# G from split operands in row tiles beside the first MLP, hi and lo of w4 in one matmul, and w4's pages in order of use

## The chip, the cores and the metric

The kernel runs on one core of one Trainium2 chip. The time is the device time of one execution in microseconds; for the kernel before it is the median of three runs. The engines of the core are named as in the profile: PE (TensorE, with its weight loads as PEld), DVE (VectorE), ACT (ScalarE), POOL (GpSimd) and SP (the queue that issues the DMAs).

## The reference

Attention reads between tokens and a small state, both ways, and then two MLPs over all 4352 tokens (8 batches of 512 tokens and 32 state rows, 512 wide).

```python
scores = scale * np.matmul(x, state.transpose(0, 1, 3, 2))      # B=8, H=8, S=512, Ns=32, D=64
a = softmax(scores)
xread = np.matmul(a, state)
a2 = softmax(scale * np.matmul(state, x.transpose(0, 1, 3, 2)))
sread = np.matmul(a2, x)
x = concat([xread, sread], axis=2)            # to 4352 x 512
h = np.maximum(x @ moe_w_in, 0.0)             # 512 -> 2048
x = h * h @ moe_w_out                         # 2048 -> 512
h = x @ moe2_w_in                             # 512 -> 2048
return (h * (1.0 / (1.0 + np.exp(-h)))) @ moe2_w_out
```

The four weight matrices arrive as 64-bit floats and are converted on the chip from their words.

## The kernel before, in words

**Accuracy.** A product of two float32 matrices is built from operands split into a hi part (rounded to the matmul type fp32r) and a lo part (the rest): hi x hi, hi x lo and lo x hi, three matmuls. `split_into` makes the parts, the hi cast on ACT and the subtraction on DVE or POOL. A few small products are done as plain F32 matmuls instead, which take longer per column.

**Order.** The kernel is written as a list of operations in class `Plan`: each call on an engine is recorded with its operands, the dependences are derived, and a greedy list scheduler orders each engine's instructions by urgency with costs from `cost` and by the slot in which the operation was recorded. Every recorded call is made in one helper, so all instructions have the line L185 in the profile; tiles tell them apart. The tiles live in 50 pages of 128x1024 floats, 10 quads of 128x512 floats, and eight banks of the accumulator memory, two each of psA, psB, psC and psD (`BA` to `BD` in the code).

**Stages.** (1) The words of a weight pair (`c_load`, `c_abs`, `c_bits`) become a float32 page by `c_sum`, or hi and lo by `c_split`. (2) The attention read xread is folded into the first MLP: `g_unit` computes G = state x w_in for a quarter q of the 2048 columns and a pair of heads, in 16 units (two for each of the eight pairs of w1); it writes G of the first two batches straight into their pages `Glo`, the rest to memory, from where `G_load` brings it back. (3) `scores` makes the attention scores; for the first three batches (b < NB = 3) as F32 matmuls against `sblkf`, a block diagonal copy of the state that `s_put` fills; for later ones from split parts. Softmax and transposes run on DVE and ACT and give AT, split into AThi and ATlo. (4) The first MLP runs in slots, one slot for a batch j and a chunk c of 128 of the 2048 columns: `gemm1` (six matmuls of 512 columns into psC, from G and AT), relu and square in `chain_a` (tile gact), and two slots later `gemm2` (twelve matmuls into psA and psB). The first three batches run their chunks 0 to 7 first and then 8 to 15, so that the conversion of the weights can keep up. The last slots serve the state rows, for which `w1_load` brings w1 back from memory and splits it. (5) The second MLP uses the seven products of Strassen and Winograd: `gemm3` in five units of tokens with four steps pp each, through silu to the tensors t in memory, and `gemm4` for pairs q of token blocks (q = 0 to 7, and a half pair 8).

**gemm4 before.** The operand tiles `g..hi`, `g..lo` (loaded and split by `g_op`, for pair q, product i and half h) are the stationary side, the pages w4 (hi and lo next to each other, 256 columns each) stream. For each of the products 1, 6, 2, 7, 5, 4, 3, each token block b of the pair and each of eight chunks k, three matmuls of 256 columns are issued, g hi with w hi, g hi with w lo and g lo with w hi, all into one half of a bank. The banks alternate with q. Products 1 and 2 share bank psA: the sum of product 1 is copied to the tile u (ACT) before product 2 adds to the same bank; DVE adds the rest into u and into the output tiles z0 and z1, which SP stores.

**Pages of w4.** `w4_load(pp)` loads all seven product pages of row block jj = pp ahead of step pp of the last gemm3 unit; they are split inside gemm4's first pair.

Of the kernel before, what the change touches and what calls it, by code (L numbers as in the profile page):

```python
# [27 lines left out]
class Plan:  # L28
# [78 lines left out]
    def cost(self, eng, method, writes, reads, args):  # L107
# [12 lines left out]
        if eng == "pe":  # L120
            n = 1
            for d in writes[0].shape[1:]:
                n *= d
            if method == "transpose":
                return 109
            share = 4 if args.get("tile_position") else 1
            return max(n / 2.4 + 13, 109) * (4 if args["rhs"].dtype == F32 else 1) / share
# [249 lines left out]
def attn_moe_moe_kernel(  # L377
# [46 lines left out]
    w1_d = [dram_tile([P, 1024], f"w1d{i}") for i in range(NC // 2)]  # L424
# [3 lines left out]
    g_d = [[dram_tile([4, P] + k + [512], f"g{i}{q}") for i, k in enumerate(([], [2]))] for q in range(4)]  # L428
# [129 lines left out]
    st = plan.tile(pages, [P, 4, 4, 2, NS], F32, "page", "st")  # L558
    sblk = [page(f"sblk{i}") for i in range(2)]
    sblkf = [quad(f"sblkf{b}") for b in range(NB)]  # L560
# [3 lines left out]
    def st_of(b, r):  # L564
        return st[r * 64:(r + 1) * 64, b // 2, :, b % 2].rearrange("p (g l) n -> p g l n", l=2)
# [10 lines left out]
    def s_put(b, dst, a):  # L576

        v = dst.rearrange("p (g a c) -> p g a c", g=2, a=4)
        for r in range(2):
            ps = slice(r * 64, (r + 1) * 64)  # L580
            copy(v[ps, :, a, r * NS:(r + 1) * NS], st_of(b, r))

# [3 lines left out]
    def g_unit(i):  # L586
        q, p = divmod(i, 4)
        g, l = divmod(p, 2)
        pg = w1p[("w1", i // 2)][:, i % 2 * 512:(i % 2 + 1) * 512]
        for bp in range(0, 4, 2):  # L590
            ts = [acc_tile(bp), acc_tile(bp + 1)]
            for k in range(2):
                for r in range(2):
                    ps, co = slice(r * 64, (r + 1) * 64), 64 * (r ^ k)
                    T.matmul(out=ts[k][co:co + 64], lhsT=st[ps, bp + k, p].rearrange("p e n -> p (e n)"),
                             rhs=pg[ps], start=True, stop=True, tile_position=(r * 64, co))
            o2 = page(f"go{i}{bp}", F32).rearrange("p (k f) -> p k f", k=2)
            for k in range(2):
                copy(o2[:, k], ts[k])
            if bp == 0:  # L600
                for b in range(2):
                    if (b, q) not in gp:
                        gp[(b, q)] = [None, page(f"Glo{b}{q}")]
                    for r in range(2):
                        D.dma_start(f32(gp[(b, q)][1])[l * 64 + r * NS:l * 64 + (r + 1) * NS, g * 512:(g + 1) * 512],
                                    o2[r * 64 + b * NS:r * 64 + (b + 1) * NS, 0])
                D.dma_start(g_d[q][0][p], o2[:, 1])
            else:
                D.dma_start(g_d[q][1][p], o2)

    def w1_store(i):
        D.dma_start(w1_d[i], w1p.pop(("w1", i)))

    def w1_load(i):
        w1p[("s", i)] = split_page(f"w1s{i}", 1024, lambda lo: D.dma_start(lo, w1_d[i]))

    def G_load(b, q):
        lo = page(f"Glo{b}{q}")
        bp, e = divmod(b, 2)
        src = g_d[q][1][:, :, bp % 2] if bp > 1 else g_d[q][0]  # L620
        for l in range(2):
            for r in range(2):
                ro = (r ^ bp % 2) * 64 + e * NS
                po = l * 64 + r * NS
                D.dma_start(f32(lo)[po:po + NS].rearrange("p (g f) -> p g f", g=2),
                            src.rearrange("(g l) x f -> l x g f", l=2)[l, ro:ro + NS])
# [21 lines left out]
    def scores(b, g):  # L648
# [280 lines left out]
    def w4_load(jj):  # L929

        w4p[jj] = {}
        for i in SEQ4:
            w4p[jj][i] = page(f"w4{jj}_{i}")
            lo = f32(w4_views(w4p[jj][i])[1])
            if SRC_B[i] in (11, 12, 21, 22):
                w4_quarter(jj, SRC_B[i], lo)
            else:
                D.dma_start(lo, w4s_d[(SRC_B[i], jj)].rearrange("p (k c) -> p k c", k=2))
# [360 lines left out]
```

## Time and profile before

| | us |
|---|---|
| median of three runs | 1395.72 (1394.1 to 1396.98) |
| the profiled execution, its own time | 1396.56 |
| its span in the trace | 1394.8 |
| PE busy | 1350.0 (97%) |
| DVE busy | 1006.7 (72%) |
| ACT busy | 693.0 (50%) |
| mean granted clock of PE | 0.991 of full speed |

The span begins with the first instruction of the profile and ends with the last; the run's own time is 1.76 us longer. Busy times overlap each other. The profile's windows give busy time per engine for a stretch; the timeline gives each instruction's start, its length and, in brackets, how long its engine was idle before it and which instruction ended that; for pipelined matmuls the distance of two starts tells the pace, not the length.

### The profile page before, as it was taken

What the parts mean: (1) busy time and instruction counts of PE and PEld (TensorE: products, weight loads), DVE (VectorE), ACT (ScalarE), POOL (GpSimd) and SP (SyncE); (2) the same over time, 40 slices, a digit from 0 to 9 for tenths busy, and PEclk for the clock granted to TensorE, in tenths of its full rate; (3) what the DMA queues carried; (4) which work ended last, traced back from release to release, by engine and by line L of the source; (5) the groups of instructions that cost most, each with busy time, mean ns of one, the idle gap of its engine ahead of it and who ended that gap; (6) DMA issues with size and microseconds to landing.
All of it is one profiled execution on the core that took longest, in us unless ns stands there. A gap on an engine that the chain in (4) does not pass through costs nothing. (4 is left out here: it accounts for less than half of the span.)

```text
span 1394.8 us, 21037 instructions
## 1 busy us (share of the span) xinstructions
PE 1350.0 (97%) x7820; PEld 1169.2 (84%) x7820; DVE 1006.7 (72%) x1524; ACT 693.0 (50%) x1070; POOL 44.8 (3%) x42
## 2 busy tenths in 40 slices
PE   5889999999999999999999999999999999999998
PEld 1557688888888888888988889998879999999998
DVE  7898598878888888885997768677876455444443
ACT  6765776556555555554743424245563343333331
POOL 1000001100000000000020000000010000000000
PEclk9999999999999999999999999999999999999999
DMA  8841844535454535452759758678897566655664
GB/s 308 313 178 63 296 155 129 165 122 166 152 168 125 176 118 162 138 191 73 256 190 355 276 209 285 216 242 295 303 345 242 197 212 227 209 178 188 196 189 113
DMA packets 206965, 283.19 MB, mean 203 GB/s; under 512 B 13456, under 2 KB 148112, under 8 KB 206864
## 3 DMA queue, kind: packets, MB, share of 16 engines
q1 hardware_dynamic: 206864, 281.86, 60.7%
q8 instruction: 61, 1.00, 0.3%
q14 instruction: 40, 0.33, 0.1%
HBM read 161.35 MB, written 116.26 MB: 199 GB/s over the span
## 5 line engine op out<-in xcount | busy, mean ns | idle before, releaser
L185 ACT ACTIVATE rg<-psC 128x512 f32<-128x512 f32 (+1 forms) x144 | 82.6, 574 | 197.4 <-PE psC L185 195.4
L185 DVE TENSOR_TENSOR gact<-rg,gact 128x512 fp32r<-128x512 f32 (+1 forms) x139 | 90.8, 655 | 20.4 <-ACT rg L185 14.6
L185 PE MATMUL psC<-AThi,Ghi 128*128 128x512 f32 x256 | 100.9, 400 | 2.3 <-ACT rg L185 2.0
L185 PE MATMUL psC<-AThi,Glo 128*128 128x512 f32 x256 | 101.2, 401 | 1.6 <-DVE Glo L185 1.6
L185 PE MATMUL psC<-ATlo,Ghi 128*128 128x512 f32 x256 | 100.5, 397 | 1.9 <-DVE ATlo L185 1.9
L185 ACT ACTIVATE gact<-rg 128x512 fp32r<-128x512 f32 (+1 forms) x144 | 87.7, 609 | 7.6 <-DMA g<-go 4.1
L185 DVE TENSOR_TENSOR rg<-rg 128x512 f32<-128x512 f32 (+1 forms) x66 | 43.7, 662 | 50.5 <-ACT rg L185 50.3
L185 PEld LDWEIGHTS psC<-AThi,Ghi 128*128 128x128 f32 x256 | 48.1, 188 | 15.7 <-ACT rg L185 2.4
L185 PEld LDWEIGHTS psC<-AThi,Glo 128*128 128x128 f32 x256 | 48.2, 188 | 14.6 <-issue 2.1
L185 PEld LDWEIGHTS psC<-ATlo,Ghi 128*128 128x128 f32 x256 | 48.3, 189 | 13.8 <-DVE ATlo L185 2.6
L185 ACT ACTIVATE r<-r 128x1024 f32<-128x1024 f32 (+2 forms) x20 | 18.6, 932 | 62.9 <-DVE r L185 52.7
L185 DVE TENSOR_SCALAR cv<-cv 128x1024 f32<-128x1024 f32 (+1 forms) x64 | 43.3, 685 | 8.0 <-ACT cv L185 7.7
L185 ACT ACTIVATE rg<-rg 128x512 f32<-128x512 f32 (+1 forms) x78 | 46.3, 594 | 0.0
L185 ACT ACTIVATE cv<-raw 128x512 f32<-128x512 f32 x64 | 40.6, 667 | 7.3 <-DMA raw<-in_w_dram 6.3
L185 DVE SCALAR_TENSOR_TENSOR cc<-raw,cv 128x512 int32<-128x512 int32 x64 | 41.8, 683 | 3.3 <-DMA g<-go 3.1
L185 DVE SCALAR_TENSOR_TENSOR cv<-raw,cv 128x512 f32<-128x512 uint32 x64 | 41.6, 683 | 0.2
L185 DVE TENSOR_TENSOR W<-psC,U 128x512 f32<-128x512 f32 (+2 forms) x40 | 24.1, 609 | 22.5 <-PE psC L185 22.2
L185 PE MATMUL psA<-cc,st 64*64 64x512 f32 x128 | 26.1, 687 | 14.6 <-DVE cc L185 14.6
L185 DVE TENSOR_TENSOR Glo<-Glo,Ghi 128x1024 fp32r<-128x1024 f32 x31 | 37.7, 1215 | 1.2 <-ACT Ghi L185 1.0
L185 ACT ACTIVATE W<-W 128x1024 f32<-128x1024 f32 (+2 forms) x20 | 18.7, 933 | 39.6 <-DVE W L185 35.7
L185 ACT ACTIVATE r<-psA 128x512 f32<-128x512 f32 (+2 forms) x40 | 20.7, 534 | 33.3 <-PE psA L185 25.6
L185 ACT CAST Ghi<-Glo 128x1024 fp32r<-128x1024 f32 x32 | 33.5, 1045 | 1.2 <-DMA Glo<-go 1.2
(1244 smaller groups left out, 4587.2 us busy)
## 6 DMA issues: line engine op xcount, KB each, us to landing
raw<-in_w_dram SPq DMA_DIRECT2D x64, 512.0 KB, 6.2
t<-s SPq DMA_DIRECT2D x36, 512.0 KB, 5.1
Glo<-g SPq DMA_DIRECT2D x96, 128.0 KB, 4.3
t<-r SPq DMA_DIRECT2D x24, 512.0 KB, 4.5
xTr<-in_xT_dram SPq DMA_DIRECT2D x16, 512.0 KB, 7.6
g<-go SPq DMA_DIRECT2D x16, 512.0 KB, 5.2
xnr<-in_xN_dram SPq DMA_DIRECT2D x16, 512.0 KB, 5.2
x<-yt SPq DMA_DIRECT2D x32, 256.0 KB, 4.1
```

The source lines that it names most:

```text
L185: lambda engine=engine, method=method, a=a, k=k: getattr(engine, method)(*a, **k)))
```

## The change

**G.** The units multiply split parts of the state (`sthi`, `stlo`, made by the new `st_split`) with hi and lo of w1 (`c_split` in place of `c_sum`): three fp32r row-tile matmuls of 64 rows, 128 columns of weights (four batches side by side) and 512 columns for each of the two heads, which lie in the two row halves of the array. Units of quarter 0 use psA and psB, the others the two psD banks. w1 is stored and reloaded as hi and lo. The pairs of w1 get the slots -6, -4, 0, 1, 12, 14, 16, 18.

**Scores** of the first three batches are F32 tile matmuls of 64x32 straight from the state; `s_put` and `sblkf` are gone.

**gemm4** streams hi and lo of w4 in one matmul of 512 columns, and g lo with w hi in a second of 256. The two token blocks use the two banks of a name. The halves of 256 are joined by an extra addition on DVE or POOL.

**w4's pages** are loaded in the order of the products, seven after each step of the last gemm3 unit. The planner's cost of tile matmuls is changed too.

```diff
     def g_unit(i):
-        pg = w1p[("w1", i // 2)][:, i % 2 * 512:(i % 2 + 1) * 512]
-        for bp in range(0, 4, 2):
-            ts = [acc_tile(bp), acc_tile(bp + 1)]
-            for k in range(2):
+        hi, lo = (t[:, i % 2 * 512:(i % 2 + 1) * 512] for t in w1p[("w1", i // 2)])
+        for bq in range(2):
+            ts = (BA, BB)[bq] if q == 0 else [att_tile(), att_tile()]
+            for k, (sw, w) in enumerate(((sth, hi), (stl, hi), (sth, lo))):
                 for r in range(2):
-                    ps, co = slice(r * 64, (r + 1) * 64), 64 * (r ^ k)
-                    T.matmul(out=ts[k][co:co + 64], lhsT=st[ps, bp + k, p].rearrange("p e n -> p (e n)"),
-                             rhs=pg[ps], start=True, stop=True, tile_position=(r * 64, co))
+                    ps = slice(r * 64, (r + 1) * 64)
+                    T.matmul(out=ts[r], lhsT=sw[ps, bq, p].rearrange("p b n -> p (b n)"),
+                             rhs=w[ps], start=k == 0, stop=k == 2, tile_position=(r * 64, 0))
...
+    def st_split():
+        split_into(*(t.rearrange("p q a b n -> p (q a b n)") for t in (sth, stl, st)))
...
     def w1_load(i):
-        w1p[("s", i)] = split_page(f"w1s{i}", 1024, lambda lo: D.dma_start(lo, w1_d[i]))
+        w1p[("s", i)] = page(f"w1s{i}hi"), page(f"w1s{i}lo")
+        for k, t in enumerate(w1p[("s", i)]):
+            D.dma_start(f32(t), w1_d[i][k])
...
         if b < NB:
             for l in range(2):
-                c0 = (2 * g + l) * P
-                T.matmul(out=t, lhsT=sblkf[b][:, c0:c0 + P], rhs=x[:, l * 512:(l + 1) * 512],
-                         start=l == 0, stop=l == 1)
+                for r in range(2):
+                    h, ps = 2 * l + r, slice(r * 64, (r + 1) * 64)
+                    T.matmul(out=t[h * NS:(h + 1) * NS], lhsT=st[ps, b // 4, 2 * g + l, b % 4],
+                             rhs=x[ps, l * 512:(l + 1) * 512], start=True, stop=True, tile_position=(r * 64, h * NS))
...
-                    for m, (g, o) in enumerate(((hi, 0), (hi, 256), (lo, 0))):
-                        T.matmul(out=bank[:, b * 256:(b + 1) * 256], lhsT=g[:, ks], rhs=w[:, o:o + 256],
-                                 start=first and b + k + m == 0, stop=last and k == 7 and m == 2,
-                                 skip_group_check=True)
+                    T.matmul(out=banks[b], lhsT=hi[:, ks], rhs=w,
+                             start=first and k == 0, stop=False, skip_group_check=True)
+                    T.matmul(out=banks[b][:, 0:256], lhsT=lo[:, ks], rhs=w[:, 0:256],
+                             start=False, stop=last and k == 7, skip_group_check=True)
...
+        def add(o, banks, a):
+            for b in range(c):
+                V.tensor_tensor(out=o[:, b], in0=banks[b], in1=a[:, b], op=ALU.add)
+
+        def join(z, a):
+            arith(ALU.add, z, a[:, :, 0:256], a[:, :, 256:512])
...
-        prod(3, bC, False, True)
-        add(z[0][:, :, hs], bC, U)
+        prod(3, BC, False, True)
+        add(U, BC, U)
+        join(z[0][:, :, hs], U)
         store(0, z[0])
...
-            n = slot(NB - 1, PARTS[part - 1][0]) + 1
-            k = n - 9 + 2 * p
-        sched_conv(("w1", i), w_in_pair(w1, i), k, w1p, whole=True)
+        n = (-6, -4, 0, 1, 12, 14, 16, 18)[i]
+        k = n - 3
+        sched_conv(("w1", i), w_in_pair(w1, i), k, w1p)
...
+            gemm3(u, pp)
             if u + 1 == NU:
-                if pp == 3:
-                    g_op(0, 1)
-                w4_load(pp)
-            gemm3(u, pp)
+                for i, jj in [(i, jj) for i in SEQ4 for jj in range(4)][7 * pp:7 * pp + 7]:
+                    w4_load(i, jj)
```

How the order moves is shown at three places.

PE at the second half of G: before, the end of its lump in the first half of batch 2 (cc is the float32 page of w1, st the state; "x2" are instructions that read alike).

```order
L185 MATMUL psB1_217<-cc_352,st_222 64x512 x2
L185 MATMUL psA0_214<-cc_364,st_222 64x512 x2
L185 MATMUL psA1_215<-cc_364,st_222 64x512 x2
L185 MATMUL psB0_216<-cc_364,st_222 64x512 x2
L185 MATMUL psC0_218<-AThi2_378,Ghi20_382 128x512
L185 MATMUL psB1_217<-cc_364,st_222 64x512 x2
L185 MATMUL psA0_214<-cc_364,st_222 64x512 x2
L185 MATMUL psA1_215<-cc_364,st_222 64x512 x2
L185 MATMUL psB0_216<-cc_364,st_222 64x512 x2
L185 MATMUL psB1_217<-cc_364,st_222 64x512 x2
L185 MATMUL psC0_218<-AThi2_378,Glo20_360 128x512
L185 MATMUL psA0_214<-gact_389,hi('w2', 0)_298 128x512
```

After, the units of w1's pair 4 beside batch 1 (sthi and stlo are the parts of the state).

```order
L187 MATMUL psD1_221<-hi('w1', 4)_369,sthi_223 128x512
L187 MATMUL psB1_217<-gact_362,hi('w2', 1)_316 128x512
L187 MATMUL psD1_221<-hi('w1', 4)_369,stlo_224 128x512
L187 MATMUL psD0_220<-hi('w1', 4)_369,sthi_223 128x512
L187 MATMUL psD1_221<-lo('w1', 4)_370,sthi_223 128x512
L187 MATMUL psD0_220<-hi('w1', 4)_369,stlo_224 128x512
L187 MATMUL psC1_219<-AThi1_333,Ghi11_358 128x512
L187 MATMUL psD0_220<-lo('w1', 4)_370,sthi_223 128x512
L187 MATMUL psC1_219<-AThi1_333,Glo11_292 128x512
L187 MATMUL psA0_214<-gact_367,hi('w2', 1)_316 128x512
L187 MATMUL psC1_219<-ATlo1_334,Ghi11_358 128x512
L187 MATMUL psA0_214<-gact_367,lo('w2', 1)_317 128x512
```

What was one lump of 64 tile matmuls in four-fold groups, broken by single matmuls of gemm1, is 96 row-tile matmuls that stand alone or in small blocks between matmuls of gemm1 and gemm2, spread over the slots 12 to 18 where the lump stood in slot 17.

PE in gemm4, before, as product 1 of pair 4 begins beside product 4 of pair 3:

```order
L185 MATMUL psA0_214<-w40_1_1308,g410hi_1489 128x256
L185 MATMUL psD1_221<-w43_4_1359,g341hi_1480 128x256
L185 MATMUL psA0_214<-w40_1_1308,g410hi_1489 128x256
L185 MATMUL psD1_221<-w43_4_1359,g341lo_1479 128x256
L185 MATMUL psA0_214<-w40_1_1308,g410lo_1488 128x256
L185 MATMUL psD1_221<-w43_4_1359,g341hi_1480 128x256
L185 MATMUL psA0_214<-w40_1_1308,g410hi_1489 128x256
```

And after, beside product 3 of pair 3:

```order
L187 MATMUL psA0_214<-w40_1_1330,g410hi_1516 128x512
L187 MATMUL psC1_219<-w40_3_1379,g330lo_1505 128x256
L187 MATMUL psA0_214<-w40_1_1330,g410lo_1515 128x256
L187 MATMUL psC1_219<-w41_3_1380,g330hi_1506 128x512
L187 MATMUL psA0_214<-w40_1_1330,g410hi_1516 128x512
L187 MATMUL psC1_219<-w41_3_1380,g330lo_1505 128x256
L187 MATMUL psA0_214<-w40_1_1330,g410lo_1515 128x256
```

Three matmuls of 256 columns per weight pair have become one of 512 and one of 256, and product 1 of the next pair begins beside the last product of the one before, on the other bank name.

SP at the same end of pair 3 (z0 is the tile numbered 1485 before and 1509 after), before:

```order
L185 DMA out_0_dram<-z1_1486 128x2x512
L185 DMA g450lo_1504<-t54_195 128x4x256
L185 DMA g451lo_1506<-t54_195 128x4x256
L185 DMA g440lo_1508<-t44_190 128x4x256
L185 DMA out_0_dram<-z0_1485 128x2x512
L185 DMA g441lo_1510<-t44_190 128x4x256
L185 DMA g430lo_1512<-t34_185 128x4x256
L185 DMA g431lo_1514<-t34_185 128x4x256
L185 DMA g510lo_1519<-t14_175 128x4x256
```

After:

```order
L187 DMA out_0_dram<-z1_1510 128x2x512
L187 DMA g450lo_1531<-t54_195 128x4x256
L187 DMA g451lo_1533<-t54_195 128x4x256
L187 DMA g440lo_1535<-t44_190 128x4x256
L187 DMA g441lo_1537<-t44_190 128x4x256
L187 DMA out_0_dram<-z0_1509 128x2x512
L187 DMA g430lo_1539<-t34_185 128x4x256
L187 DMA g431lo_1541<-t34_185 128x4x256
L187 DMA g510lo_1549<-t14_175 128x4x256
```

The store of z0 has moved past the load of g441 and is directly ahead of g430.

## Rows read from the trace of the kernel before

**Rows 1.** The page, busy time, share of the span and instructions of each engine.
```profile
PE 1350.0 (97%) x7820; PEld 1169.2 (84%) x7820; DVE 1006.7 (72%) x1524; ACT 693.0 (50%) x1070; POOL 44.8 (3%) x42
```

**Rows 2.** The timeline of PE in gemm4: start us, length us, engine, operation, names.
```profile
1125.26 0.28 PE L185 MATMUL psB<-w,g260hi 128*128 128x256 f32 x1
...
1126.94 0.28 PE L185 MATMUL psB<-w,g261lo 128*128 128x256 f32 x1
```

**Rows 3.** The timeline of PE in the first MLP.
```profile
63.06 0.39 PE L185 MATMUL psC<-AThi,Ghi 128*128 128x512 f32 x1
...
63.74 0.39 PE L185 MATMUL psC<-ATlo,Ghi 128*128 128x512 f32 x1
```

**Rows 4.** Waits of PE from 1100 us to the end: total us, times, longest.
```profile
PE psA L185 <- ACT u L185: 4.7, 5, 2.0
```

**Rows 5.** The timeline of all engines around the end of pair 3 in gemm4.
```profile
1207.40 0.68 DVE L185 TENSOR_TENSOR z<-psC,u 128x512 f32<-128x512 f32 x1
...
1209.25 1.30 SPq L185 DMA_DIRECT2D g430lo<-t  x1
...
1218.59 1.04 ACT L185 CAST g430hi<-g430lo 128x1024 fp32r<-128x1024 f32 x1 [0.29 <-DMA g430lo<-t]
1219.54 0.58 ACT L185 COPY u<-psA 128x512 f32<-128x512 f32 x1
...
1220.17 0.39 PE L185 MATMUL psA<-w,g420hi 128*128 128x256 f32 x1 [2.04 <-ACT u L185]
```

**Rows 6.** The timeline of PE in gemm4's first pair.
```profile
1044.85 0.50 PE L185 MATMUL psC<-w,g050hi 128*128 128x256 f32 x2 [1.75 <-ACT g050hi L185]
1048.89 0.58 PE L185 MATMUL psD<-w,g070lo 128*128 128x256 f32 x1 [3.54 <-DVE g070lo L185]
```

**Rows 7.** Windows: length, busy us (instructions) per engine, PEclk, DMA share, GB/s.
```profile
80.00:100.00 20.00, 15.02 (x51) 10.43 (x50) 19.99 (x35) 8.23 (x16) 0.92 (x2) 0.83 0.31 100
1025.00:1050.00 25.00, 19.16 (x130) 17.55 (x129) 18.25 (x22) 14.94 (x18) 0.00 (x0) 0.94 1.06 369
```

**Rows 8.** The timeline of PE from 80 to 126 us, where it waited.
```profile
83.15 0.73 PE L185 MATMUL psA<-gact,hi('w2', 2)_327 128*128 128x512 f32 x2 [1.25 <-DVE gact L185]
...
87.84 1.06 PE L185 MATMUL psC<-AThi,Glo 128*128 128x512 f32 x2 [1.60 <-DVE Glo L185]
90.78 1.22 PE L185 MATMUL psC<-ATlo,Ghi 128*128 128x512 f32 x2 [1.88 <-DVE ATlo L185]
...
124.82 0.73 PE L185 MATMUL psA<-gact,hi('w2', 2)_327 128*128 128x512 f32 x2 [1.91 <-DVE gact L185]
```

**Rows 9.** The timeline of PE in the lump of G's second half.
```profile
135.73 1.09 PE L185 MATMUL psA<-cc,st 64*64 64x512 f32 x8
136.64 1.02 PE L185 MATMUL psB<-cc,st 64*64 64x512 f32 x4
137.60 0.50 PE L185 MATMUL psC<-AThi,Ghi 128*128 128x512 f32 x1
138.03 0.65 PE L185 MATMUL psB<-cc,st 64*64 64x512 f32 x2
138.04 0.65 PE L185 MATMUL psA<-cc,st 64*64 64x512 f32 x2
...
154.65 0.50 PE L185 MATMUL psC<-AThi,Glo 128*128 128x512 f32 x1
```

**Rows 10.** The timeline of weight loads there.
```profile
137.59 0.19 PEld L185 LDWEIGHTS psC<-AThi,Ghi 128*128 128x128 f32 x1 [0.81 <-issue]
...
154.75 0.19 PEld L185 LDWEIGHTS psA<-gact,hi('w2', 0)_298 128*128 128x128 f32 x1
```

**Rows 11.** The page, a group of DVE: count, busy us, mean ns.
```profile
L185 DVE TENSOR_TENSOR Glo<-Glo,Ghi 128x1024 fp32r<-128x1024 f32 x31 | 37.7, 1215 | 1.2 <-ACT Ghi L185 1.0
```

**Rows 12.** Waits of DVE from 0 to 125 us.
```profile
DVE go L185 <- PE psA L185: 3.2, 1, 3.2
```

**Rows 13.** The timeline of DVE at the end.
```profile
1390.27 0.42 DVE L185 TENSOR_TENSOR z<-psC,u 128x256 f32<-128x256 f32 x1 [1.37 <-PE psC L185]
```

More of the change, by code (lines that the diff above doesn't have):

```diff
@@ L125, in cost @@
                 return 109
[L126 to L127 removed]
+            if not args.get("tile_position"):
+                return max(n / 2.4 + 13, 109) * (4 if args["rhs"].dtype == F32 else 1)
+            return n / 2.4 * 1.8 if args["rhs"].dtype == F32 else n / 4.4
         if eng == "act":
@@ L555, in w_out_pair @@
         return [w.bitcast(I32)[c * P:(c + 1) * P, :] for c in (2 * i, 2 * i + 1)]
-    st = plan.tile(pages, [P, 4, 4, 2, NS], F32, "page", "st")
+    st = plan.tile(pages, [P, 2, 4, 4, NS], F32, "page", "st")
+    sth, stl = (plan.tile(pages, [P, 2, 4, 4, NS], F32R, "page", f"st{k}") for k in ("hi", "lo"))
     sblk = [page(f"sblk{i}") for i in range(2)]
-    sblkf = [quad(f"sblkf{b}") for b in range(NB)]
     ident = plan.tile(const, [P, P], F32, "ident", "ident")
@@ L574, in s_build @@
             split_into(hi, lo, src)
[L576 to L581, printed above, removed]
     w1p, gp = {}, {}
@@ L927, in w4_views, with w4_load @@
         return v[:, 0], v[:, 1]
[L929 to L938, printed above, removed]
+    def w4_load(i, jj):
+        w4p[(jj, i)] = page(f"w4{jj}_{i}")
+        lo = f32(w4_views(w4p[(jj, i)])[1])
+        if SRC_B[i] in (11, 12, 21, 22):
+            w4_quarter(jj, SRC_B[i], lo)
+        else:
+            D.dma_start(lo, w4s_d[(SRC_B[i], jj)].rearrange("p (k c) -> p k c", k=2))
     def w4_split(jj, i):
-        hi, lo = w4_views(w4p[jj][i])
+        hi, lo = w4_views(w4p[(jj, i)])
         split_into(hi, lo, f32(lo))
@@ L1044, in gemm4, with prod @@
         c = 2 if q < B else 1
-        n = c * 256
-        def prod(i, bank, first, last):
+        def prod(i, banks, first, last):
             if q == 0:
@@ L1074, in store @@
                     D.dma_start(out[r0:r0 + NS, :], z[i * NS:(i + 1) * NS, 0, :])
-        bA, bB, bC, bD = (t[q % 2] for t in (BA, BB, BC, BD))
-        z = [page(f"z{t}", F32)[:, :c * 512].rearrange("p (b d) -> p b d", b=c) for t in range(2)]
+        z = [new(f"z{t}") for t in range(2)]
         ls, hs = slice(0, 256), slice(256, 512)
-        prod(1, bA, True, False)
-        u = page("u4", F32)
-        U, W = (part(u[:, i * 512:(i + 1) * 512]) for i in range(2))
-        A.copy(U, part(bA))
-        prod(6, bB, True, True)
-        add(U, bB, U)
-        prod(2, bA, False, True)
-        A.copy(z[0][:, :, ls], part(bA))
-        prod(7, bD, True, False)
-        add(W, bD, U)
-        prod(5, bC, True, False)
-        add(z[1][:, :, hs], bC, W)
-        prod(4, bD, False, True)
-        add(z[1][:, :, ls], bD, U)
+        prod(1, BA, True, False)
+        U = new("U4")
+        for b in range(c):
+            A.copy(U[:, b], BA[b])
+        prod(6, BB, True, True)
+        add(U, BB, U)
+        prod(2, BA, False, True)
+        R = new("R4")
+        for b in range(c):
+            A.copy(R[:, b], BA[b])
+        join(z[0][:, :, ls], R)
+        prod(7, BD, True, False)
+        W = new("W4")
+        add(W, BD, U)
+        prod(5, BC, True, False)
+        add(W, BC, W)
+        join(z[1][:, :, hs], W)
+        prod(4, BD, False, True)
+        X = new("X4")
+        add(X, BD, U)
+        join(z[1][:, :, ls], X)
         store(1, z[1])
-        prod(3, bC, False, True)
-        add(z[0][:, :, hs], bC, U)
+        prod(3, BC, False, True)
+        add(U, BC, U)
+        join(z[0][:, :, hs], U)
         store(0, z[0])
```

53 lines of the change are left out of this document (21 added, 32 removed).

## The prediction, made before the run

> **What bounds the kernel now.** I read the page first: TensorE (PE) is busy 1350.0 of 1394.8 us [rows 1], so a microsecond is won either by issuing less PE work or by closing the 44.8 us in which PE stands idle. Then I looked at where these two lie. In gemm4 PE starts one 256-column matmul after the other [rows 2], as in the first MLP with 512 columns [rows 3]: PE sets the pace, and a wait of 4.7 us in five pieces is all that shows in the last 295 us [rows 4]. The longest of them opens the second use of bank A: ACT casts g430hi, the copy of U stands behind that cast, and PE waits 2.04 us for the copy [rows 5]. Between gemm3 and gemm4 PE waits 1.75 and 3.54 us for the operands of products 5 and 7 [rows 6], while the DMA engines are full (1.06) and the clock averages 0.94 [rows 7]. At the beginning it is the other way round: from 80 to 100 us DVE is busy 19.99 of 20 us and PE 15.02, at a clock of 0.83 [rows 7], and PE waits for DVE's results four times up to 125 us, 6.64 us together [rows 8]. After that PE is the limit, and the second half of G stands there as one lump from 135.73 to 154.65 us [rows 9].
>
> **Part 1, gemm4.** For each batch pair, 7 products x 2 token blocks x 8 chunks = 112 groups of three 256-column matmuls become 112 groups of one 512-column and one 256-column matmul; the columns stay the same. A 256-column matmul takes 0.120 us from start to start (14 steps from 1125.26 to 1126.94 [rows 2]), a 512-column one 0.227 (three steps from 63.06 to 63.74 [rows 3]). The 256 columns between them cost 0.107, so a matmul has about 0.0133 us over its columns: 0.120 - 0.107. Each group saves one of these: 3 x 0.120 - (0.227 + 0.120) = 0.0133 us, a pair 112 x 0.0133 = 1.49 us, and the whole gemm4 (eight pairs and one half) 8.5 x 1.49 = 12.7 us. In the first pair PE waits for loads [rows 6], so a faster PE there only waits longer; I count 7.5 pairs, **-11.2 us**.
> The Trainium skill (TensorE: Matmul & The Clock Gate, Back-to-back issue gap) gives an isolated matmul N/2.4 + 2.5 ns; by its 2.5 ns the 952 groups would save 2.4 us, not 12.7. The rows show 13 ns, and the measurement decides.
>
> The price is more evacuation. Evacuations of 512 columns double in number (ACT 0.58, DVE 0.68 each [rows 5]) and four joins per pair are new; DVE is busy for 72% of the whole span [rows 1] and has the room. What matters is the end of a pair: z0 now needs a second add and a join before its store, and the loads behind this store on SP come later by about 0.6 us more (one 0.68 add, less what overlaps). Against this, before, the load of g441 stood between the store and g430 (1207.40 the add, 1209.25 the issue of g430); now g441 goes ahead of the store. The two cancel within a microsecond, so I leave the U waits as they are: **0**, bounds -4.7 (all gone [rows 4]) and +4.8 (0.6 in each of eight pairs).
>
> **Part 2, G.** Before, a half unit is four F32 quadrant matmuls in 0.91 us (135.73 to 136.64 [rows 9]); the lump of eight units holds 16 of them and five single full-array matmuls. To its last single matmul it lasts 154.65 - 135.73 = 18.92 us; less four full ones of 0.227, G costs 18.0 us. Afterwards these eight units are 96 row-tile matmuls of 64 rows and 512 columns. Two that lie in different row halves can run together: at 138.03 us the old tiles begin in pairs 0.01 apart [rows 9]. But the new order scatters them in 54 blocks (37 are single matmuls) among 146 full-array ones. With pairs inside a block taking 0.227, the blocks hold 70 slots: 70 x 0.227 = 15.9 us.
> Each block also changes the array between tiles and full width twice. The trace has this: the single full matmul begins 0.96 after the half-finished group before it, where 0.91 is usual, and the next tile begins 0.43 after it, where 0.227 is usual [rows 9]. So a change there and back costs 0.05 + 0.20 = 0.25 us. It is the only such price in the trace, for F32 tiles; bounds 0 and 0.25 + 0.19, the 0.19 being a weight load that starts only with its own matmul (137.59) where between full ones it starts 0.2 ahead (154.75) [rows 10]. I take 0.25: 54 x 0.25 = 13.5 us. Together 29.4 us against 18.0, **+11.4 us**. Cover: half of the new units sit three to five slots earlier, where PE now waits for DVE; 6.64 us of waits [rows 8] can take them up, and the clock there (0.83) can only gain. I count 6.6, which leaves **+4.8**. Bounds: with free changes 15.9 - 18.0 - 6.6 = -8.7, and with 0.44 and no cover 15.9 + 23.8 - 18.0 = +21.7.
> The Trainium skill (TensorEngine Tiling (Array Packing), Key Properties) says that changing the tiling mode drains TensorE; the rows agree with 0.20 us, and it speaks against scattering G.
>
> **Part 3, start.** Pairs of w1 are now split into hi and lo: one more cast on ACT and one more 128x1024 subtraction on DVE each, 1.22 us [rows 11]; st is split too. Four pairs and st ahead of the first batches make 5 x 1.22 = 6.1 us for DVE. Against this, pairs 2 and 3 are converted later, the copies of s_put go, and DVE has waits of its own, one of them 3.2 us for PE [rows 12], that more work can fill. Scores as tiles, and the first half of G (12 blocks), lie beside DVE's work. I take **+1**, bounds -4 (two conversions moved out of the way) and +6.1. The stores and reloads of w1 double (8 x 512 KB twice); they lie where PE waits for nothing, **0**.
>
> **Part 4, w4 pages.** They now come in the order of use, seven after each gemm3 step of the last unit. Loads for the first pair stand behind the last seven. The best is that the two waits and the lost clock go (1.75 + 3.54, and 0.06 x 25 = 1.5: -6.8); the worst is that seven half pages of 256 KB at the 369 GB/s of [rows 7], 5 us, go ahead of what PE waits for. **0**, with both ends kept.
>
> **Part 5, the end.** The last add of the half pair was 0.42 us [rows 13]; now it is a 512-column one (0.68) and then a 0.42 join: **+0.7**.
>
> Sum: -11.2 + 0 + 4.8 + 1 + 0 + 0.7 = **-4.7 us**. The profiled execution took 1396.56 us (1.76 over its span), so it would come to 1396.6 - 4.7 = 1391.9; it lies 0.84 above the median of the runs, and the forecast for the median is 1395.7 - 4.7 = **1391.0 us**. A measurement of this kernel can tell about 0.2% (2.8 us) from no change.
>
> **The rivals.**
> *A: the changes are cheap.* Weight loads of fp32r tiles could be hidden in the other row half. Then G is -8.7, and the sum -11.2 - 8.7 + 1 + 0.7 = -18.2: 1377.5; if the transition's waits go as well, 1371. For it: tiles in different halves do begin together. Against: 0.43 where 0.227 is usual [rows 9].
> *B: the changes cost more than counted, the time rises.* The place is the 54 blocks between chunk 4 of batch 1 and batch 2. If each change also exposes a weight load (0.25 + 0.19 = 0.44), G is 15.9 + 54 x 0.44 - 18.0 - 6.6 = +15.1 and the sum +5.6: 1401. It decides from a price at which G eats the 9.5 us of the rest: (9.5 + 18.0 + 6.6 - 15.9)/54 = 0.34 us a block. For it: loads at the change start with their matmul [rows 10]. Against: part of the 0.20 is already such a load. The drain that the Trainium skill names (TensorEngine Tiling (Array Packing), Key Properties) would be such a mechanism.
> *C: the end of each pair eats gemm4's saving.* If the chain add, join, store, loads, cast, U is what sets a pair's length, PE just waits 1.5 us longer each time: the sum is 4.8 + 1.7 = +6.5: 1402. For it: the U waits come in five of eight pairs. Against: 4.7 us in all is less than 1 us a wait, and three pairs have none [rows 4].
> *D: two row tiles do not run together.* Then the change does not do "two heads at once": 96 x 0.227 = 21.8 instead of 15.9, +5.9, the sum +1.2: 1397.
>
> **How the numbers follow.** Forecast 0.42 (faster 0.35, same 0.07), A 0.16 (faster), B 0.21 (same 0.04, slower 0.17), C 0.12 (same 0.02, slower 0.10), D 0.09 (faster 0.02, same 0.07). Faster 0.53, same 0.20, slower 0.27. The range 1376 to 1404 goes from A to B and C with 2 us of a slower start; left out are A with the transition's waits gone and B without cover. The likeliest case alone is 1386 to 1395.
>
> **What would show it.** A pair of gemm4 in the new trace lasts 1.5 us less, start to start, with waits for the U copy of at most 2 us. Between slots 12 and 20 a full matmul next to a row tile shows a step of about 0.4 us; two row tiles begin within 0.02 us. PE's idle time before 125 us shrinks. I am wrong if gemm4 as a whole is less than 8 us shorter, if the stretch up to the end of batch 2's first part is no longer or more than 10 us longer, or if the transition moves by more than 5 us.

## The result: slower by 1%, with 25 us lost at the start and 14 won at the end

| | before | after |
|---|---|---|
| median, us | 1394.91 (1393.72 to 1396.98, 4 runs) | 1410.92 (1407.22 to 1411.71, 4 runs) |
| ratio | 1 | 1.010 (95%: 1.0082 to 1.0117) |
| span of the profiled execution, us | 1394.8 | 1405.4 |

In a later series the changed kernel came to 1405.31 us against 1397.44, a ratio of 1.0062 (1.0042 to 1.0082). Its eight executions lie between 1403.3 and 1411.7 us, and the profiled one is the fastest of the first four; the trace therefore shows 10.6 of the 16 us. The forecast was 1391.0 us. In the series of experiment 6 one execution each of two kernels took 2026.03 and 2230.19 us at granted clocks of 0.617 and 0.559, and the figures given there are without them.

The page of the changed kernel, busy time and the clock in 40 slices, answers to [rows 1]:

```profile
PE 1369.8 (97%) x6828; PEld 1124.4 (80%) x6828; DVE 1052.5 (75%) x1594; ACT 705.4 (50%) x1086; POOL 50.9 (4%) x41
...
PEclk9699999999999999999999999999999999999999
```

PE is busy 19.8 us longer, with a thousand instructions fewer. Where the 10.6 us come from is read best by landmarks that both traces have: the first matmul of a slot of the first MLP (two matmuls psC<-AThi,Ghi a slot, so the 25th opens slot 12), of a gemm3 unit, of product 2 of a pair. Starts in us, from the timelines of PE:

| landmark | before | after | difference |
|---|---|---|---|
| slot 0 | 45.20 | 48.09 | +2.9 |
| slot 4 | 54.67 | 75.53 | +20.9 |
| slot 12 | 106.87 | 115.61 | +8.7 |
| slot 24 | 178.13 | 203.33 | +25.2 |
| slot 127 | 643.93 | 668.86 | +24.9 |
| gemm3, last unit | 952.98 | 980.76 | +27.8 |
| pair 1, product 2 | 1095.76 | 1116.75 | +21.0 |
| pair 7, product 2 | 1344.28 | 1354.65 | +10.4 |
| last matmul | 1389.95 | 1399.52 | +9.6 |
| end of the span | 1394.79 | 1405.43 | +10.6 |

So 8.7 us are lost before slot 12, 16.5 between slots 12 and 24 (the second half of G), 2.9 in gemm3; then 6.8 are won back from the last gemm3 unit to pair 1 and 10.6 in six pairs of gemm4. Landmarks at the start vary from execution to execution: in three traces with the start of before slot 12 begins between 106.75 and 108.45 us, in three with the new start between 114.11 and 115.61, so the 8.7 stands for 5.7 to 8.9. The stretch from slot 12 to 24 does not vary: 71.25 to 71.30 and 87.72 us in the same traces.

**The second half of G.** The timeline of PE in the changed kernel as the units of pair 4 begin (to be held against the lump of [rows 9]):

```profile
117.87 0.39 PE L187 MATMUL psC<-ATlo,Ghi 128*128 128x512 f32 x1
118.19 0.50 PE L187 MATMUL psD<-hi('w1', 4)_369,sthi 64*128 64x512 f32 x1
118.62 0.49 PE L187 MATMUL psA<-gact,hi('w2', 1)_316 128*128 128x512 f32 x1
119.05 0.49 PE L187 MATMUL psD<-hi('w1', 4)_369,sthi 64*128 64x512 f32 x1
119.05 0.73 PE L187 MATMUL psD<-hi('w1', 4)_369,stlo 64*128 64x512 f32 x2
119.39 0.39 PE L187 MATMUL psD<-lo('w1', 4)_370,sthi 64*128 64x512 f32 x1
119.71 0.50 PE L187 MATMUL psA<-gact,lo('w2', 1)_317 128*128 128x512 f32 x1
120.14 0.50 PE L187 MATMUL psD<-lo('w1', 4)_370,sthi 64*128 64x512 f32 x1
120.57 0.50 PE L187 MATMUL psA<-gact,hi('w2', 1)_316 128*128 128x512 f32 x1
120.91 0.40 PE L187 MATMUL psB<-gact,hi('w2', 1)_316 128*128 128x512 f32 x1
```

From a full-width matmul to a tile 0.32 us pass (117.87 to 118.19), from a tile to a full-width one 0.43 (118.19 to 118.62), and the full-width one that follows it at last, 120.57 to 120.91, takes 0.34. Against 0.227 each, a block costs 0.093 + 0.203 + 0.113 = 0.41 us beside its own work, not the 0.25 of the forecast. (The way into a block and the way out of it are called its passages below.) Single steps differ, 0.32 or 0.43 us on either side; but PE waits for nothing between slots 12 and 24, so the whole stretch can be added up: 87.72 us less 219 full-width matmuls and 70 slots of tiles, each 0.227, leaves 22.1 us for 54 blocks, 0.41 each. Tiles of two row halves do begin together (119.05 twice).

**The start.** Busy times of the changed kernel by window (length; busy and count for PE, PEld, DVE, ACT, POOL; clock; DMA share; GB/s):

```profile
20.00:40.00 20.00, 15.19 (x52) 7.47 (x51) 13.58 (x21) 14.09 (x26) 0.00 (x0) 0.84 0.71 244
30.00:32.00 2.00, 1.17 (x6) 0.63 (x5) 1.28 (x3) 1.89 (x4) 0.00 (x0) 1.00 0.27 66
36.00:38.00 2.00, 0.08 (x2) 0.08 (x2) 2.00 (x4) 1.33 (x3) 0.00 (x0) 0.50 1.00 358
40.00:60.00 20.00, 19.19 (x51) 10.39 (x49) 16.45 (x29) 11.79 (x21) 0.00 (x0) 0.56 0.84 276
60.00:80.00 20.00, 20.00 (x77) 11.29 (x76) 15.01 (x20) 13.56 (x23) 0.00 (x0) 1.00 0.84 262
100.00:120.00 20.00, 19.16 (x80) 14.32 (x80) 19.73 (x30) 12.72 (x23) 0.00 (x0) 1.00 0.14 56
140.00:160.00 20.00, 19.97 (x66) 10.69 (x65) 7.89 (x12) 9.60 (x17) 0.00 (x0) 1.00 0.44 147
```

DVE is full from 100 to 120 us (19.73 of 20), as it was before [rows 7]; but from 60 to 80 us PE is full and DVE is not (15.01), so DVE does not set the pace all the way to slot 12. From 40 to 60 us PE has a mean clock of 0.56; in 30:32 it was busy 1.17 of 2 us, in 36:38 for 0.08 us, and then stands at 0.50. From 140 to 160 the row shows PE full and DVE at 7.89: there PE is the bound, as in the lump of before. What holds DVE up at the start is seen on two engines. PE first:

```profile
17.25 1.91 PE L187 MATMUL psD<-xTr,st 64*32 64x512 f32 x2
19.09 0.80 PE L187 MATMUL psA<-lo('w1', 0)_239,sthi 64*128 64x512 f32 x2
...
20.25 1.92 PE L187 MATMUL psD<-xTr,st 64*32 64x512 f32 x4
```

A single score tile (x2: its two records) holds PE from 17.25 to 19.09, 1.84 us; the next two together hold it as long (20.25 to the next start at 22.09). DVE has a copy of G at the head of its queue, and PE's matmuls for it stand behind those tiles; it waits 6.42 us:

```profile
30.72 0.69 DVE L187 COPY go<-psA 128x512 f32<-128x512 f32 x1 [6.42 <-PE psA L187]
```

**gemm4.** The pace of two products side by side, in answer to [rows 2]:

```profile
1204.42 0.40 PE L187 MATMUL psD<-w,g371hi 128*128 128x512 f32 x1
1204.65 0.40 PE L187 MATMUL psC<-w,g350hi 128*128 128x512 f32 x1
1204.89 0.28 PE L187 MATMUL psD<-w,g371lo 128*128 128x256 f32 x1
1205.00 0.27 PE L187 MATMUL psC<-w,g350lo 128*128 128x256 f32 x1
1205.12 0.40 PE L187 MATMUL psD<-w,g371hi 128*128 128x512 f32 x1
```

The step after a 512-column matmul is 0.23 us, after a 256-column one 0.12: as worked out. The waits for U from 1095 us on are 3.2 us in four, where [rows 4] had 4.7 in five:

```profile
PE psA L187 <- ACT U L187: 3.2, 4, 1.2
```

In the first pair, the operands of product 7 now cost 0.74 and 0.56 us where [rows 6] had 3.54, and nothing waits for g050; two waits for DVE's W are new:

```profile
1069.79 0.47 PE L187 MATMUL psD<-w,g070hi 128*128 128x512 f32 x1 [0.74 <-ACT g070hi L187]
...
1071.41 0.50 PE L187 MATMUL psD<-w,g070lo 128*128 128x256 f32 x2 [0.56 <-DVE g070lo L187]
...
1089.33 0.47 PE L187 MATMUL psD<-w,g040hi 128*128 128x512 f32 x1 [1.32 <-DVE W L187]
...
1092.53 0.50 PE L187 MATMUL psD<-w,g040hi 128*128 128x512 f32 x1 [1.33 <-DVE W L187]
```

The end, in answer to [rows 13], has a longer add and the join, 1.07 us more from the last matmul to the end of the span:

```profile
1399.83 0.69 DVE L187 TENSOR_TENSOR U<-psC,U 128x512 f32<-128x512 f32 x1 [0.35 <-PE psC L187]
1400.55 0.42 DVE L187 TENSOR_TENSOR z<-U 128x256 f32<-128x256 f32 x1
```

### The profile page after: what moved, and what is told of

It is laid out like the page before. It is cut to its first block, busy times and chain, and to the rows that moved or that the text cites. A ratio compares the mean times of both kernels' runs of the same rounds, so it can differ in the third digit from the quotient of the medians.

```text
span 1405.4 us, 19137 instructions
## 1 busy us (share of the span) xinstructions
PE 1369.8 (97%) x6828; PEld 1124.4 (80%) x6828; DVE 1052.5 (75%) x1594; ACT 705.4 (50%) x1086; POOL 50.9 (4%) x41
## 5 line engine op out<-in xcount | busy, mean ns | idle before, releaser
L187 DVE TENSOR_TENSOR W<-psD,U 128x512 f32<-128x512 f32 (+2 forms) x57 | 35.4, 630 | 35.4 <-PE psD L187 35.3
L187 DVE TENSOR_TENSOR U<-psB,U 128x512 f32<-128x512 f32 (+2 forms) x57 | 34.9, 628 | 15.1 <-PE psB L187 13.7
L187 ACT COPY go<-psD 128x512 f32<-128x512 f32 x43 | 24.5, 588 | 32.8 <-PE psD L187 30.5
L187 ACT COPY U<-psA 128x512 f32<-128x512 f32 (+2 forms) x57 | 29.2, 540 | 19.7 <-PE psA L187 18.9
```

The lines of the kernel that those rows point to most:

```text
L187: lambda engine=engine, method=method, a=a, k=k: getattr(engine, method)(*a, **k)))
```

## The experiments

**1. Start and end apart.** Three kernels: the new gemm4 and page order with the old start; the new start with the old gemm4 and page order; the new gemm4 alone. Each takes whole functions from one kernel or the other, for the last one:

```diff
 # kernel before
-    def gemm4(q): ...            # three matmuls of 256 columns
+    def gemm4(q): ...            # one of 512, one of 256, joins
```

> The kernel before with the new gemm4 and the new page order, all of the start (G, scores, w1) as before. Theory (start and end add up, the start loses about 25 us, the end wins about 17): gemm4 saves 10 to 11 us, the step from gemm3 to gemm4 about 7, the last add and join cost 1: 1376 to 1380 us. Rival (the gain at the end is only the late start made up, since loads have more time ahead): 1385 to 1395 us.

> The changed kernel with the gemm4 and the page order of before. Theory (start and end add up): slot 24 of the first MLP begins 25 us later than before, and all of it stays: 1416 to 1423 us. Rival (the late start is partly made up in gemm3 and gemm4): 1400 to 1410 us.

> The kernel before with the new gemm4 alone, page order as before. Theory (TensorE's pace, 1.5 us per pair): 1383 to 1386 us, and the waits between gemm3 and gemm4 stay at 5 us. Rival (the step from gemm3 to gemm4 gains through the new gemm4, not the page order): 1376 to 1380 us.

Measured: old start 1379.51 us, ratio 0.9883 (0.9855 to 0.9911); new start 1421.76, ratio 1.0176 (1.0139 to 1.0213); gemm4 alone 1380.91, ratio 0.9888 (0.9858 to 0.9917). Start and end add up: +26.5 and -15.7 against 1395.23 make +10.8, between the +16.0 and +7.9 that the two series show for the whole change. The page order by itself does nothing that can be told (1379.5 with it, 1380.9 without): the third run ended 0.9 us above the range of its rival and 2.1 below that of its theory, and the step between gemm3 and gemm4 gains through the new gemm4, as the rival had it. In the old start's trace pair 1 to pair 7 (starts of product 2) wins 15.88 - 6.93 = 8.95 us in six pairs, 1.49 each.

**2. G in pieces.** The six matmuls of a half unit become one operation of the planner, so that nothing is put between them.

```diff
-            for k, (sw, w) in enumerate(((sth, hi), (stl, hi), (sth, lo))):
+            def mm(ts=ts, bq=bq):
+                for k, (sw, w) in enumerate(((sth, hi), (stl, hi), (sth, lo))):
...
+            plan.together("pe", mm)
```

> The changed kernel with the six row-tile matmuls of a half unit of G put out as one piece. Theory (each block of tiles among full-width matmuls costs 0.41 us): 54 blocks in the second half become 16, 38 x 0.41 = 15.6 us less, and 70 slots become 48, 5.0 us less; a little is lost to waits for the accumulator banks: 1391 to 1399 us. Rival (the time goes into the copies out of the two psD banks, whatever the order): within 4 us of the changed kernel, 1406 to 1414 us.

Measured: 1390.39 us, ratio 0.9959 (0.9941 to 0.9978), 0.6 us below the range. Slot 12 begins 2.5 us later than in the changed kernel's trace. Slots 12 to 24 take 186.40 - 118.11 = 68.3 us, 19.4 less than in the changed kernel and 3.0 less than before; the expectation was 20.6. The timeline shows one piece with one passage in and one out:

```profile
128.04 0.39 PE L188 MATMUL psC<-ATlo,Ghi 128*128 128x512 f32 x1
128.36 0.50 PE L188 MATMUL psD<-hi('w1', 4)_369,sthi 64*128 64x512 f32 x2
128.69 0.40 PE L188 MATMUL psD<-hi('w1', 4)_369,stlo 64*128 64x512 f32 x2
128.93 0.39 PE L188 MATMUL psD<-lo('w1', 4)_370,sthi 64*128 64x512 f32 x2
129.25 0.50 PE L188 MATMUL psA<-gact,lo('w2', 1)_317 128*128 128x512 f32 x1
129.59 0.40 PE L188 MATMUL psB<-gact,hi('w2', 1)_316 128*128 128x512 f32 x1
```

0.32 us into it, three pairs and the passage out in 0.89 (128.36 to 129.25), 0.34 after it. Less the 5.0 us for concurrency, 14.4 us fell with 38 blocks: 0.38 us a block, close to the 0.41 read from the rows.

**3. What is lost before slot 12.** First the scores as before, then the first four pairs at their old slots and banks.

```diff
 # changed kernel; run 1
-            T.matmul(out=t[h * NS:(h + 1) * NS], lhsT=st[ps, b // 4, 2 * g + l, b % 4], ...)
+            T.matmul(out=t, lhsT=sblkf[b][:, c0:c0 + P], rhs=x[:, l * 512:(l + 1) * 512], ...)
 # changed kernel; run 2
-        n = (-6, -4, 0, 1, 12, 14, 16, 18)[i]
+        n = (-10, -8, -6, -4, 12, 14, 16, 18)[i]
-            ts = (BA, BB)[bq] if q == 0 else [att_tile(), att_tile()]
+            ts = (BA, BB)[bq] if q < 2 else [att_tile(), att_tile()]
-            at(-9, "vec", st_split)
+            at(-12, "vec", st_split)
```

> The changed kernel with the scores of the first three batches as before (full-width F32 against the block diagonal copy, with its copies and memsets). Theory 1 (the 8.7 us that are lost before slot 12 come from score tiles set singly between blocks of G, which hold PE and with it DVE's copy of G): slot 12 begins 4 to 6 us earlier than in the changed kernel, 1403 to 1407 us in all. Theory 2 (they come from quarter 1 of G, which waits for copies out of only two psD banks at half the clock): no more than 2 us.

> The changed kernel with the first four pairs of w1 at the slots of before (-10 to -4), their G in psA and psB. Theory 2 (two psD banks and half the clock beside slots 0 to 3): slot 12 begins within 2 us of the kernel before, 1400 to 1404 us in all. Theory 1 (score tiles between blocks of G): slot 12 stays 6 us or more later than before, within 3 us of the changed kernel.

Measured: old scores 1400.62 us, slot 12 at 110.95, 4.7 us earlier, as theory 1 had it (3.2 earlier than in the repeated kernel of experiment 5; the total is 2.4 below the theory's range). The old slots gave 1418.75 us and slot 12 at 128.62, 13 us later: neither theory said that. The trace has theory 1's cause in a stronger form. PE, and then DVE:

```profile
22.61 1.91 PE L187 MATMUL psD<-xTr,st 64*32 64x512 f32 x2
24.45 0.79 PE L187 MATMUL psA<-hi('w1', 0)_238,stlo 64*128 64x512 f32 x1
```

```profile
40.68 0.69 DVE L187 COPY go<-psB 128x512 f32<-128x512 f32 x1 [17.21 <-PE psB L187]
```

Eight score tiles stand singly between G tiles there from 17 to 39 us, 1.84 us each, and DVE's copy of G waits 17.21 us for psB. All of them run at the lower level of the clock: pairs of row tiles keep a step of 0.43 us until 44.70 us here, until 26.95 in the changed kernel. How much of the 13 us is this late rise was not tried.

**4. All of G at the old place.** Split G at the old slots in psA and psB, without and with pieces (the edits of 2 and 3, for all pairs).

> The changed kernel with all of G from split operands at the slots and in the banks (psA, psB) of before. Theory (a block of tiles costs 0.41 us, work in pairs 0.227): the lump has 19 blocks and 56 slots, 20.5 us against 18.0 before; with up to 4 us at the start, 1381 to 1386 us. Rival (split operands cost as much as their place: more DVE and ACT work at the start, doubled stores): 1390 us or more.

> The same as the lump, with the six matmuls of a half unit put out as one piece. Theory: 11 blocks and 48 slots, 4.5 + 10.9 = 15.4 us against 18.0 before, so 3 us less than the old F32 lump and 5 less than the run before this one, if the copies of two banks per 0.68 us keep up: 1376 to 1381 us. Rival (ACT and DVE need 0.58 us for each of 32 copies, so the lump is bound by them): no faster than the ungrouped lump.

Measured: 1415.26 and 1390.77 us. Both theories missed; the first run's rival fits its number, the second's does not. At slot 12 the first has the same delay as the run with the old slots (128.19), the second begins it 15.1 us earlier (113.08); and from slot 12 to 24 they need 81.7 and 76.7 us, not 74 and 69. Windows of the two kernels, in which PE is busy for only 13 of 20 us:

```profile
140.00:160.00 20.00, 13.06 (x44) 9.37 (x43) 19.53 (x34) 6.47 (x13) 0.00 (x0) 0.85 0.37 142
```

```profile
120.00:140.00 20.00, 13.70 (x55) 9.81 (x53) 20.00 (x32) 10.82 (x18) 0.00 (x0) 0.89 0.47 172
```

DVE is full: the four conversions of the second half, each now with one pass more, fall close together (in the first of the two their lo parts begin at 136.57, 137.68, 151.08 and 152.21 us). Spread conversions take less time from slot 12 to 24, 68.3 us against 76.7 where both have pieces; but the lump begins slot 12 5.0 us earlier, and the two totals, 1390.39 and 1390.77 us, can't be told apart. What is shown is that matmuls spread one by one cost more than pieces: in pieces, the lump gains 24 us over the ungrouped one, the 15.1 before slot 12 among them.

**5. Score tiles in pieces too.** The four tiles of a group as one operation, in the run with the old slots and in the run with G's pieces, and G's pieces with the old scores; and the changed kernel once more.

> The run with the first four pairs at the old slots, but the four score tiles of a group put out as one piece. Theory (a lone F32 score tile between G tiles holds PE 1.84 us, as long as four together; nine of them held up DVE's copy of G for 17.2 us): the wait is gone, slot 12 begins 10 to 16 us earlier, within 8 us of the kernel before; 1402 to 1409 us in all. Rival (the late start is the DVE and ACT work of the split): slot 12 gains less than 5 us, 1413 us or more.

> The changed kernel with both put out as pieces, the six matmuls of a half unit of G and the four score tiles of a group. Theory: the score tiles cost the start 5 us more when scattered; 1383 to 1387 us, against 1390.4 with G's pieces alone. Rival: within 2 us of 1390.4.

> The changed kernel with G in pieces and the scores as before (full-width F32). Theory (the two findings add: 4.7 us before slot 12 from the scores, 19 us after it from G's pieces): 1380 to 1386 us. It beats old gemm4's best partner, the old start at 1379.5, only if split G in pieces is worth more than the extra splitting on DVE. Rival: 1388 us or more.

> The changed kernel once more, beside the others. The profiled execution of the result was the fastest of its four by 3.6 us. Theory (the start differs from run to run, in the length of the stretch at half the clock): span 1405 to 1410 us, the difference lies before slot 12, gemm4 within 1 us. Rival (gemm4's waits vary): the difference lies after slot 127.

Measured: 1404.94, 1386.65, 1386.33 (0.3 above its range) and 1405.31 us. With score tiles in pieces slot 12 begins at 114.44 instead of 128.62 (old slots) and at 114.33 instead of 118.11 (G's pieces): lone score tiles are shown as a cause. (G's pieces alone had put slot 12 later, so 114.33 is no earlier than the 114.11 of the repeated kernel.) Together G's pieces and tiles in pieces take 18.7 us off the changed kernel in this series. In all of these slot 12 still begins 7.2 to 7.6 us later than before. The repeated kernel's profile is 1.5 us earlier at slot 12 and loses 3.4 us after it, 1.9 of them between the product 2 of pairs 3 and 5 and 1.2 behind the last matmul: neither theory on the spread holds, both places vary.

**6. The remaining 7 us.** c_split makes the lo part of w1 in two passes of DVE; here in one, as many as c_sum had. The last bits of w1's words are left out of the computation. Once with G's pieces and the old scores, once in the changed kernel; and, as a control, the old start with its F32 G in pieces.

```diff
     def c_split(key, into):
-        split_into(hi, c, c)
-        arith(ALU.add, lo, c, a)
+        if key[0] == "w1":
+            split_into(hi, lo, c)
+        else:
+            split_into(hi, c, c)
+            arith(ALU.add, lo, c, a)
```

> The run with G in pieces and the scores as before, but the lo part of w1 is made by one subtraction on DVE, as many 128x1024 passes as the kernel before; the last bits of the 64-bit words of w1 (the small second part of the conversion) are left out of the computation. Theory (what is left of the late start, 7.2 us at slot 12, is the second DVE pass of 1.22 us for each pair of w1): slot 12 begins 4 to 7 us earlier, 1379 to 1383 us in all. Rival (it is ACT's casts, the psD banks or the half clock): less than 2 us earlier, 1384 us or more.

> The changed kernel with the same single DVE pass for w1's lo part (the last bits of w1's words left out). Theory: the DVE pass and the scattered matmuls add, so slot 12 gains 3 to 6 us, from 114 to 116 us to 109 to 112, and slots 12 to 24 stay about 87 us long as long as the blocks stay scattered: 1400 to 1405 us. Rival: no gain at slot 12.

> The kernel before with the new gemm4 and page order, and its F32 G put out in pieces of a half unit (four quadrant matmuls). Theory (a passage costs 0.41 us there and back, and a broken half unit its concurrency): the lump has 13 pieces' passages where it had 6, but whole ones; within 3 us of the old start, 1377 to 1383 us. Rival (F32 pieces gain as the split ones do, 15 us): 1370 us or less.

Measured: 1378.00 us (ratio 0.9880, 0.9862 to 0.9898; 1.0 below its range), slot 12 at 108.84, 5.2 us earlier: the second pass is most of the rest. In the changed kernel it missed: 1409.39 us and slot 12 at 122.75, since the planner set other score tiles singly, and DVE waited up to 9.5 us for psD. F32 pieces changed nothing (1378.81 us against 1379.51): the old lump had few passages to lose.

**The best versions** are the old start with the new gemm4 and page order, 1379.5 us, and split G in pieces with one DVE pass, 1378.0 but without w1's last bits; 1.5 us apart in different series, they can't be told apart. Both beat the kernel before by 1.2%.

## Why the prediction was wrong

**Part 1 was right.** 0.0133 us for each matmul saved, 1.49 us a pair. It is best seen where PE waits for nothing at the full clock; there the 112 groups of a pair (from the start of one to the start of the 113th) take 40.43 us before and 38.90 after, 1.53 less:

```profile
1329.14:1369.57 40.43, 40.43 (x338) 40.37 (x337) 17.47 (x20) 12.54 (x16) 0.00 (x0) 1.00 0.53 164
```

```profile
1221.61:1260.51 38.90, 38.90 (x225) 33.97 (x224) 26.02 (x28) 17.09 (x19) 0.00 (x0) 1.00 0.67 218
```

That the six pairs with the old start also show 1.49 is luck: those stretches hold waits and, before, 3.4 us at half clock from 1221.3 us on, and the same six pairs took 236.92 to 240.25 us in the kernels with the new gemm4 against 248.52 before, 1.4 to 1.9 a pair.

**Part 2 failed in the price of a passage.** "So a change there and back costs 0.05 + 0.20 = 0.25 us" was read around F32 quadrant tiles; around fp32r row tiles it is 0.41. The term before cover becomes 15.9 + 54 x 0.41 - 18.0 = +20.0 instead of +11.4. The rows of [rows 10] had it in sight: the weight load that starts only with its own matmul was kept for a bound. The cover was wrong as well: three of the four waits that were to take up 6.64 us (4.73 us of them) stand before slot 12 [rows 8], where none of these units comes. Between slots 12 and 24 the kernel before has the fourth, 1.91 us, and 3.4 us at half clock from 125.6 us on, which cost half of that, 1.7: 3.6 together, and 20.0 - 16.5 = 3.5 were there. The stretch before adds up to the same: 218 full-width matmuls of 0.227, 18.0 for G, 1.91 and 1.7 make 71.1 of 71.26 us. This is rival B, with its price of 0.44 and its point of decision at 0.34.
The Trainium skill's rule on the drain (TensorEngine Tiling (Array Packing), Key Properties) spoke against the change, and the result bears it out. The Trainium skill's rule that weight loads overlap with running matmuls only when the row group differs (TensorE: Matmul & The Clock Gate, Part 3) fits two halves that begin together and the loads beside a tile that begin with their own matmul; it does not fit the loads between full-width matmuls, which use the same rows and begin 0.2 us ahead [rows 10], and there the measurement decides. Whether a drain or the late load makes the 0.41 was not separated. Nor was it tried what the changed planner cost of tiles does to the order.

**Part 3 failed in "lie beside DVE's work".** +1 was forecast, +8.7 came. DVE's busy and idle time up to slot 12 say how: the kernel before, the changed kernel, and the changed kernel with the old scores:

```profile
0.00:106.87 106.87, 80.28 (x342) 46.65 (x343) 88.38 (x136) 70.26 (x124) 4.80 (x13) 0.95 0.73 261
```

```profile
0.00:115.61 115.61, 96.03 (x335) 54.31 (x335) 93.39 (x139) 73.16 (x123) 4.58 (x10) 0.90 0.75 259
```

```profile
0.00:110.95 110.95, 88.32 (x311) 57.18 (x311) 93.27 (x140) 74.33 (x128) 5.27 (x13) 0.89 0.78 270
```

Then G's pieces with the old scores, with two DVE passes and with one:

```profile
0.00:114.08 114.08, 84.05 (x310) 54.41 (x311) 94.09 (x141) 73.49 (x127) 5.28 (x13) 0.90 0.77 263
```

```profile
0.00:108.84 108.84, 83.38 (x310) 53.26 (x311) 89.49 (x138) 72.97 (x126) 4.81 (x13) 0.94 0.82 280
```

Of the 8.7 us, 5.0 are more work on DVE (93.39 against 88.38), within the bound of 6.1 but not hidden: one pass less gave 5.2 us back, 4.6 of them DVE's busy time. The other 3.7 are more idle time of DVE (22.2 against 18.5, the rest of the two lengths): PE's work was not beside DVE's. DVE's queue holds the copies that free G's banks, so a lone score tile on PE holds up DVE; the old scores leave DVE's work as it is and take 4.5 us off its idle time, at a mean clock of 0.89 against 0.90. Its waits move between G's copies and results of ACT as the order changes, so the idle time can't be put down to one of them.

**Part 4 and the first pair failed in "a faster PE there only waits longer".** From gemm3's last unit to pair 1, 6.8 us were won where 0 was taken. That this is the end of the range given for the waits going is luck. 2.2 of the 6.8 are only order: fewer matmuls of pair 1 stand ahead of its product 2 than before. Counted by work, from gemm3's last unit to the start of the 113th group of gemm4, it is 126.57 us before and 121.98 in the changed kernel, 4.6 less; 122.08 with the old start, 122.21 with gemm4 alone, and 126.76 with the new start and the old gemm4. So the new gemm4 does it without the page order. The waits of PE in this stretch did not go but moved: 5.8 us before and 4.6 after, 2.6 of them the new ones for W. The 112 groups of the first pair save 1.5 us, the waits 1.2, and the clock at most 2.6 (an estimate: before, there are 6.8 us at half clock from 1047.2 us on, PE was busy for 5.1 of them, and at full clock those take 2.6 less). The clock is seen in one window; before, gemm4 alone, and the old start with both:

```profile
1045.00:1055.00 10.00, 6.46 (x34) 6.26 (x35) 8.53 (x8) 4.67 (x5) 0.00 (x0) 0.66 1.07 391
```

```profile
1045.00:1055.00 10.00, 7.26 (x31) 6.10 (x32) 8.28 (x8) 5.03 (x6) 0.00 (x0) 0.83 1.07 392
```

```profile
1045.00:1055.00 10.00, 10.00 (x59) 8.70 (x59) 4.75 (x6) 2.43 (x5) 0.00 (x0) 1.00 1.07 392
```

0.66, 0.83 and 1.00 in the same ten microseconds, with the DMA as full in all three; in the last kernel two waits for W, 3.2 us together, come after it. Which of the new gemm4's parts moves the waits (banks by block in place of alternating ones, or the loads' order) wasn't tried and stays open.

**Part 5** was nearly right: +1.1 from the last matmul on, +0.7 forecast.

**The sum.** By the landmarks: 8.7 to slot 12, 16.5 to slot 24, -0.3 to slot 127, 2.9 in gemm3, -6.8 to pair 1, -10.6 to pair 7, -0.8 to the last matmul and 1.1 behind it are the trace's +10.6. The 2.9 in gemm3 were not forecast and not tried; the changed kernel's trace has a wait of 2.1 us for DVE's r there, 0.7 before, and 3.4 us at half clock from 760.8 us on, which the trace before has not. The sign was lost in parts 2 and 3, which are 25 us where 5.8 were forecast. The range ended at 1404 because B and C were priced with the forecast start. Two of the forecast's own signs of being wrong came: the stretch to slot 24 is more than 10 us longer, and the step from gemm3 to gemm4 moved by more than 5 us by these landmarks.

## What to carry to other kernels

Before row tiles are spread into a stream of full-width matmuls, count the passages and price them with the nearest rows on both sides of a passage: here 0.4 us for each block, nearly two full matmuls, so that one piece of six is cheap and six single ones are not. A short operation of another engine at the head of a queue (here DVE's copy out of a bank) makes that engine wait for the whole order of PE ahead of it; here work that was counted as lying beside DVE's cost DVE 3.7 us of idle time. What a gain per instruction is worth (0.0133 us each) can be read from two paces in one trace: 1.49 us a pair were worked out, and pairs without a wait show 1.53. And a wait covers new work only where both stand in the same stretch.

## What was not expected of the hardware

- A single F32 score tile of 64x32 keeps PE 1.84 us at the lower level of the clock, and two of them put out together take as long (17.25 to 19.09 and 20.25 to 22.09 in the changed kernel's timeline). At the full clock one takes 0.97 (65.22 to 66.19) and four together 0.99 (63.79 to 64.78).
- The clock column of the first 25 us says 1.00, but the pace says otherwise: pairs of row tiles there take 0.59 and 0.43 us a step (11.64 to 12.23; 26.10 to 26.53), from 26.95 on 0.23. That is the pace of the lower of the two levels; the trace's own clock records begin only at 26.9 us, and the column shows 1.00 where there are none.
- PE then had 1.00 until 33.7 us, was busy for 1.17 of 2 us at 30 to 32, and was granted 0.50 from there to 57.6 us, 23.9 us long; the kernel before has 10.2 us of it up to slot 12. What it costs wasn't tried. In the row of 40 to 60 us the work of 19.19 us at 0.56 would take about 10.7 at full clock (an estimate), so up to 8 us could be lost there; but the run with the old scores has 23.9 us of it as well and reaches slot 12 4.7 us earlier.
